# Gate and value projections without sets of seven products, and a new order around them

## The chip, the cores and the metric

The kernel runs on one core of one Trainium2 chip. The metric is the device time of one execution in microseconds; smaller is better. Times given as a median come from several runs of the same program; the profile describes one execution of its own.

## What is computed

Two layers run one after the other. The first is attention with routing by clusters, for 4 batches of 8 heads, 768 positions and a head size of 64. Each query and each key is assigned to the nearest of its head's 16 centroids, and a query sees only the keys of its own cluster:

```python
q_assign = np.argmax(np.einsum('bhsd,hcd->bhsc', q_n, c_n), axis=-1)
k_assign = np.argmax(np.einsum('bhsd,hcd->bhsc', k_n, c_n), axis=-1)
mask = q_assign[:, :, :, None] == k_assign[:, :, None, :]
scores = np.where(mask, scale * (q @ k^T), -1e9)
attn = softmax(scores);  attn_out = attn @ v
```

The second is a gated feed-forward layer over the 3072 tokens that result (512 features in and out, 1536 in between):

```python
x = attn_out.transpose(0, 2, 1, 3).reshape(3072, 512)
gate = 1.0 / (1.0 + np.exp(-(x @ w_gate)))
out = (gate * (x @ w_val)) @ w_out
```

Inputs and output are float32; inside, most products are made in float16.

## The kernel before, in words

**Tiles and stages.** Heads are handled in pairs (four pairs p a batch b), and the queries of a batch in groups (b, gr): two groups of 384 tokens for batches 1 to 3; for batch 0 a group of 256 and one of 512. The work of a pair has these steps:

- Loads of q, k and v into the `nat` tiles. For the first batch, and for the first two pairs of the second, q and k come as one plain transfer a tile (`load_nat`, last part) and are turned by TensorE against an identity matrix (L617, L795, L903); all later ones come in quarters and are turned on VectorE (L595).
- Cluster scores (L687, L835, L948), the largest of each 16 (L556), the comparison with it (L563), and the turning of the resulting one-hot rows (L574) into the augmented tiles `even` and `odd`, which hold 64 rows of q or k and 16 rows of one-hot. One product of 80 rows then gives the score and the mask at once. For the first pairs `place` writes these rows on VectorE directly.
- Attention (`attend`): scores (L1008) into one of two `sc` tiles of two banks each, the exponential on ScalarE (L1032), the product with v (L1059), which also sums the weights; then a reciprocal and a normalisation on VectorE (L1084, L1089), and the turning of the result into `x` by a transposing DMA on SP (L1117) or by TensorE and VectorE (L1097, L1113).

When all pairs of a group are done, `feed` makes the feed-forward layer's first half for that group, and `project` its second half.

**The gate and value projections.** `feed` goes over 12 feature chunks of 128. In the plain form (`proj`, L1422) each chunk has a gate product and a value product, each of four matmuls over 384 tokens into one of three `ring` banks; a tanh on ScalarE (L1585) and a gating on VectorE (L1596) follow. Two chunks so take 16 matmuls of 384 columns.

In the other form, `seven_products`, two feature chunks are made as one set. The set is seen as a product of 2 x 2 blocks: the two halves of the 512 input features against the two kinds, gate and value, and the two halves of the tokens. Seven block products with sums of blocks take the place of eight. Each has four matmuls over 192 columns (L1498), 28 a set. What this needs beside them:

- sums of weight blocks, made once for the chunk pairs 2, 4 and 8 (`sum_up_weights`, L1403, four on VectorE for each);
- differences of blocks of `x`, four on VectorE for each group with sets (L1460), kept in `tb`;
- in each set three copies out of a bank by ScalarE (L1517), three additions by VectorE (L1529), two tanh (L1536) and two gatings (L1544). Later products of a set add to a bank that an earlier product has filled and that has been copied first.

The number of sets goes by group: none in batch 0, 2 and 2 in batch 1, 2 and 3 in batch 2, 3 and 2 in batch 3. In the last group, (3, 1), the sets use `sc` tiles as banks, in the others `ring`. The plain form makes the chunks that remain.

**The projection** (`project`, L1275) uses sums and differences of blocks of its own, on the hidden tile `hT` and the output weights. The change does not touch it.

**What sets the order.** Every step is a task added with `od.add`: an engine, a planned duration, what it needs, the buffers it takes, a due time, and `lat`, the planned delay from its end until others may use its result. `Order.schedule` simulates the engines with these numbers and picks, among the tasks that can start first on an engine, the one with the earliest due time. `Order.transfers` plans the landing of DMAs. After eight rounds the tasks are issued in the planned order, and each engine and each queue then runs its instructions in that order on the chip. So a changed duration, `lat` or due time changes no work, but can change the order on every engine.

The numbers that the change touches:

- in `load_nat`, `lat` of a plain load: 2.0 for the second batch (L497);
- in `place`, the due time of the last two of the eight turned rows of pair 0: 2.0 later than the others (L765);
- in `attend`, `early`: the scores before slot 150 are due 33.5 earlier and their value products 19.5 earlier (L997); a pair and group of batches 1 to 3 has 12 slots, and batch 1 begins at slot 96;
- at the end of `attend`, the reciprocal, the normalisation and the turning of the result are due 7.0 before the block (L1122 to L1136);
- `WT` (L1647): the time from which each weight load may be issued on POOL, and its due time; the first two are those of the first third of the gate and of the value weights.

Of the kernel before, what the change touches and what calls it, by code (L numbers as in the profile page):

```python
# [209 lines left out]
def kernel(  # L210
# [64 lines left out]
    od = Order(BUFS, HEIRS)  # L275
# [17 lines left out]
    WP = (2, 4, 8)  # L293
# [50 lines left out]
    c_ident16 = od.add("POOL", 0.2, lambda: nc.gpsimd.tensor_copy(ident16, ident), [c_ident], due=8)  # L344
# [99 lines left out]
    def load_nat(b, p, nm, eng, due, early=0.0, hold=None, behind=()):  # L444
        src = {"k": k, "q": q, "v": v}[nm]
        buf = natb[b, p, nm] = Buf("late" if b else "nat")
        if isinstance(due, tuple):

            nat[b, p, nm] = []
            for e in range(2):  # L450
                nat[b, p, nm].append(
                    dma(
                        eng,
                        lambda e=e: (buf.tile if e else take(buf))[:, e, :, :],
                        lambda e=e: src[b, 2 * p + e].rearrange("(p c) d -> p c d", c=NCH),
                        0.65, (), due[e], acq=[] if e else [buf], uses=[buf] if e else [],
                        seq=nat[b, p, nm][:], lat={"k": (-0.35, -0.8), "q": (0.0, -0.2)}[nm][e],
                    )
                )
            return  # L460
        if quarters(b, p) and nm != "v":

            parts = src[b, 2 * p : 2 * p + 2].rearrange(
                "h (x t c e) (g f) -> e g t c (h x) f", t=32, c=NCH // 2, e=2, g=2
            )
            nat[b, p, nm] = []
            for a in range(4):
                nat[b, p, nm].append(
                    dma(
                        eng,  # L470
                        lambda a=a: (buf.tile if a else take(buf))[
                            32 * a : 32 * a + 32
                        ].rearrange("p h c d -> p (h c d)").rearrange(
                            "p (c x f) -> p c x f", c=NCH // 2, f=32
                        ),
                        lambda a=a: parts[a // 2, a % 2],
                        0.7 if eng == "POOL" else 0.55, (), due, acq=[] if a else [buf], uses=[buf] if a else [],
                        early=early, seq=nat[b, p, nm][:1], pkt=13, lat=2.0,
                    )
                )  # L480
            return
        held = []
        if hold:

            held.append(
                od.add(
                    "DVE", 0.07, lambda: nc.vector.memset(take(buf)[0:1, 0, 0, 0:1], 0.0), [], -8.7,
                    acq=[buf], seq=hold,
                )
            )  # L490
        nat[b, p, nm] = [
            dma(
                eng,
                lambda: buf.tile if held else take(buf),
                lambda: src[b, 2 * p : 2 * p + 2].rearrange("h (p c) d -> p h c d", c=NCH),
                1.05, held, due, acq=[] if held else [buf], uses=[buf] if held else [], early=early,
                seq=behind, lat=2.0 if b else (0.2 if p == 1 else 1.0),  # L497
            )
        ]

# [41 lines left out]
    aug, masked, shifted, turns, in_turn = {}, {}, {}, [], []  # L542
# [207 lines left out]
    def place(b, p, ohf, tiles, last, due, alloc, c):  # L750


        ev, od_ = aug[b, p]
        rows = [(0, "k", 0), (0, "q", 0), (1, "k", 0), (0, "k", 1), (0, "q", 1), (1, "k", 1)]
        if not p:
            rows += [(1, "q", 0), (1, "q", 1)]
        for n_, (e, nm, h) in enumerate(rows):
            g = tiles.index((nm, h))
            m = od.add(
                "DVE", 0.4,  # L760
                lambda g=g, e=e, nm=nm, h=h: turn_matches(
                    aug[b, p][e].tile[64:96, NM[nm], h * QB : (h + 1) * QB],
                    ohf.tile[32 * g : 32 * g + 32, 32 * e : 32 * e + QB],
                ),
                [last, *alloc], lat=0.02, due=due + 0.3 * n_ + (2.0 if n_ > 5 else 0.0), uses=[ohf, aug[b, p][e]],  # L765
            )
            masked[b, p, e, nm, h] = [c[nm, e, h], m]

        if not p:
            return  # L770
        m = dma(
            "SP", lambda: od_.tile[64:80, NM["q"], :],
            lambda: ev.tile[80:96, NM["q"], :], 0.1,
            [masked[b, p, 0, "q", h][1] for h in range(2)] + alloc, due + 20.0, uses=[ev, od_],
        )
        for h in range(2):
            masked[b, p, 1, "q", h] = [c["q", 1, h], m]
# [205 lines left out]
    def attend(block, at, slot):  # L983


        due = due_at(slot)
# [7 lines left out]
        qb_ = aug[b, p][par]  # L994
        sc, es = Buf("sc"), Buf("es")
        vp = vps[(b * NP + p) % NVP]
        early = slot < 150.0  # L997
        t1 = []
        for i, (e, j) in enumerate(some):
            kb = aug[b, p][j % 2]  # L1000

            def score(i=i, e=e, j=j, kb=kb):
# [17 lines left out]
                    acq=[] if i else [sc], uses=[kb, qb_] + ([sc] if i else []),  # L1020
                    seq=scored_last[-1:],
# [24 lines left out]
        first, last = at == 0, at + together == len(UNITS)  # L1046
        if first:
            avb[block] = Buf("av")
        av = avb[block]
# [3 lines left out]
        def value():  # L1053
# [12 lines left out]
        t3 = od.add(  # L1066
            "PE", 0.031 * together * nq,
            value, [t2] + [vload[b, p][e] for e in dict.fromkeys(e for e, _ in some)],
            due + (-4.1 if last else 5.5) - (19.5 if early else 0.0), lat=0.25 if last else 0.0,
            seq=exps[-1:], acq=[av] if first else [], uses=[es] + ([] if first else [av]),  # L1070
        )
# [6 lines left out]
        rr, xn, rg = Buf("rr"), Buf("xn"), Buf("ring")  # L1078
# [25 lines left out]
        xb, xd = x_of[b, gr], xdone[b, gr]  # L1104
# [14 lines left out]
                in_=xn.tile[:, :nq].rearrange("p c d -> p (c d)"),  # L1119
            )  # L1120

        t4 = od.add("DVE", 0.11, rec, [t3], due - 7.0, lat=0.12, acq=[rr], uses=[av])  # L1122
        t5 = od.add("DVE", 0.12 + 0.113 * nq, norm, [t4], due - 7.0, lat=0.14, acq=[xn], uses=[av, rr])
        if not ((b, gr) == (0, 0) and p >= 2 or (b, p) == (0, NP - 1) or block == blocks[-1]):

            xd.append(
                od.add(
                    "SP", 1.4, turn_by_dma, [t5], due - 7.0, seq=xd[:1], lat=0.0 if b else 5.0, dma=0.4,
                    acq=[] if xd else [xb], uses=[xn] + ([xb] if xd else []),
                )  # L1130
            )
            return together
        t6 = od.add("PE", 0.02 + 0.06 * nq, turn, [t5, c_ident16], due - 7.0, lat=0.25, acq=[rg], uses=[xn])
        xd.append(
            od.add(
                "DVE", 0.1 + 0.118 * nq, out_of_bank, [t6], due - 7.0, lat=0.14, seq=xd[:1],  # L1136
                acq=[] if xd else [xb], uses=[rg] + ([xb] if xd else []),
            )
        )
# [242 lines left out]
    wsums_of = {}  # L1382
# [9 lines left out]
    def sum_up_weights(n, fa, due):  # L1392
        g1, g2, v1, v2 = weights(fa)
        s2, s3, s4, s1 = (wss[:, n, i] for i in range(4))
        before = [wload["g"][fa // FPG], wload["v"][fa // FPG]]
        tasks = []
        for to, x, y, op in (
            (s1, v1, v2, ALU.add), (s3, g1, v1, ALU.subtract), (s2, s1, g1, ALU.subtract), (s4, g2, s2, ALU.subtract),
        ):
            tasks.append(  # L1400
                od.add(
                    "DVE", 0.4 if "DVE" == "DVE" else 1.65,
                    lambda to=to, x=x, y=y, op=op: Q2["DVE"].tensor_tensor(to, x, y, op),  # L1403
                    before + tasks[-1:], due, lat=0.12, both=True,
                )
            )
        wsums_of[fa] = [tasks[-1]]

    def feed(b, gr, work):
# [21 lines left out]

        hs_.append(hb)
        free = [h_last[hs_[-3]]] if len(hs_) > 2 else []
        seven = WP[: {(0, 0): 0, (0, 1): 0, (1, 0): 2, (1, 1): 2, (2, 0): 2, (2, 1): 3, (3, 0): 3, (3, 1): 2}[b, gr]]
        if not wsums_of:
            for n, fa in enumerate(WP):
                sum_up_weights(n, fa, 70.0 + 2 * n)
        half = N // 2
        tb, t_tasks = Buf("tb"), []

# [8 lines left out]
        if seven:  # L1449
            for n, (to, x, y) in enumerate(  # L1450
# [6 lines left out]
                def differ(to=to, x=x, y=y, n=n):  # L1457
                    if not n:
# [6 lines left out]
                        acq=[] if n else [tb], uses=[xb] + ([tb] if n else []), seq=free,  # L1465
# [107 lines left out]
        for fc in range(NFC):  # L1573
            due = due_ffn(work)
# [6 lines left out]
            rg, g1 = proj("g", fc, due, free)  # L1581
# [8 lines left out]
            due = due_ffn(work + 0.65 * w)  # L1590
            rv, v1 = proj("v", fc, due, [g1])

            def gated(fc=fc, rv=rv, gt=gt):
# [9 lines left out]
                    acq=[] if fc else [hb], uses=[gt, rv] + ([hb] if fc else []),  # L1603
# [35 lines left out]
    for p_ in range(1, NP):  # L1639
        load_nat(  # L1640
            0, p_, "k", "SP", -8 + p_, hold=[c1] if p_ == 1 else None,
            behind=nat[0, p_ - 2, "v"] if p_ > 1 else nat[0, 0, "k"],
# [1 line left out]
        load_nat(0, p_, "q", "SP", -7.9 + p_, behind=nat[0, p_, "k"])  # L1644
        load_v(0, p_ - 1, "SP", -7.8 + p_, 20.0 + 4.5 * p_, behind=nat[0, p_, "q"])
    load_v(0, NP - 1, "SP", -7.7 + p_, 20.0 + 4.5 * NP, behind=nat[0, NP - 2, "v"])
    WT = (12.5, 16.0, 23.0, 24.0, 29.5, 29.5, 38.0, 29.0, 43.0)  # L1647
    n = 0
    for i in range(NWG):
        for kind in ("g", "v"):  # L1650
# [11 lines left out]
    slot = work = 0  # L1662
# [71 lines left out]
```

## Time and profile before

| | |
|---|---|
| median of 3 runs | 315.62 us (315.27 to 318.08) |
| the profiled execution | 316.29 us |
| its span in the trace | 314.5 us |
| granted TensorE clock, mean | 0.999 |
| instructions | 8301 |

The span runs from the first to the last instruction of the trace; some 1.8 us of the profiled execution lie outside it. PE is TensorE's matmul stream and PEld its weight loads, which overlap it; DVE is VectorE, ACT ScalarE, POOL GpSimd, SP the engine that issues most transfers. A row of a group gives line, engine, operation, what it writes and reads, the shape, the count, then busy time, the mean of one in nanoseconds, and the idle time ahead of it with what ended it. A matmul's duration includes its fill and drain, which overlap the next one, so a product's cost is read from start to start.

### The profile page before, as it was taken

To read this page: it belongs to the slowest core of one execution; us is meant where nothing else is said; L and a number is where in the kernel's file an instruction comes from. 1 tells how busy PE (TensorE), PEld (TensorE's weight loads), DVE (VectorE), ACT (ScalarE), POOL (GpSimd) and SP (SyncE) were. 2 spreads that over 40 slices of the span, in tenths; PEclk is the share of its full clock that TensorE was granted. 3 is DMA by queue.
4 is the path that set the end of the run, shared out by engine and by line. 5 is a ranking of instruction groups with operands and counts; after the bars stand their busy time and mean duration, and the time that the engine had idled before them with its cause. 6 is when DMAs were issued, how large, how long until landed. Compare 5 with 4: busy or idle time off the path is not lost.

```text
span 314.5 us, 8301 instructions
## 1 busy us (share of the span) xinstructions
PE 303.7 (97%) x3251; PEld 223.0 (71%) x3251; DVE 236.5 (75%) x575; ACT 235.0 (75%) x365; POOL 77.5 (25%) x110
## 2 busy tenths in 40 slices
PE   7998899999999999999999999999999999999895
PEld 3677688644578867757776877757777888768674
DVE  4999847799978749885486978977475944786893
ACT  4799899332999979868897768957899778943521
POOL 5897563881011401340002200470000000000000
PEclk9999999999999999999999999999999999999999
DMA  6999999994465886891465683996200022000003
GB/s 216 376 273 150 238 215 121 124 147 68 82 101 105 142 137 176 105 113 40 106 102 88 104 185 94 100 122 59 83 6 15 15 81 79 16 2 36 34 0 133
DMA packets 97430, 34.49 MB, mean 110 GB/s; under 512 B 83136, under 2 KB 93296, under 8 KB 97392
## 3 DMA queue, kind: packets, MB, share of 16 engines
q1 hardware_dynamic: 72048, 24.30, 34.1%
q0 software_dynamic: 24336, 8.65, 27.1%
q10 hardware_dynamic: 1008, 1.02, 0.9%
q8 instruction: 25, 0.41, 0.5%
q14 instruction: 13, 0.11, 0.1%
HBM read 28.34 MB, written 6.29 MB: 110 GB/s over the span
## 4 chain that ended last, share of the span: by engine, by line
PE 83%; ACT 5%; DMA 5%; DVE 5%; issue 1%; DVEq 0%; SPq 0%; ACTq 0%
PE ring L1422 28%; PE sc L1008 17%; PE ring L1275 15%; PE av L1059 9%; PE ring L1498 8%; ACT es L1032 3%; PE sc L687 3%; DMA nat<-in_q_dram 3%; PE sc L1275 2%; DMA out_dram<-out 1%; PE sc L1498 1%; DMA cn<-in_centroids_dram 1%; DVE t L577 1%; DVE even L574 1%; ACT nat L1517 1%
## 5 line engine op out<-in xcount | busy, mean ns | idle before, releaser
L1032 ACT ACTIVATE es<-sc,nbias 128x768 f16<-128x768 f32 (+1 forms) x189 | 168.6, 923 | 18.4 <-PE sc L1008 17.0
L1059 PEld LDWEIGHTS <-es 128*128 128x128 f16 x1152 | 54.9, 97 | 15.0 <-issue 0.2
L1059 PE MATMUL av<-vp,es 128*128 128x65 f16 x1152 | 60.1, 193 | 0.0
L1585 ACT ACTIVATE gt<-ring 128x384 f32<-128x384 f32 (+2 forms) x68 | 34.2, 503 | 33.9 <-PE ring L1422 26.2
L1422 PE MATMUL ring<-x,wv 128*128 128x384 f16 (+2 forms) x272 | 55.3, 325 | 0.1
L1422 PE MATMUL ring<-x,wg 128*128 128x384 f16 (+2 forms) x272 | 55.4, 326 | 0.0
L1596 DVE SCALAR_TENSOR_TENSOR hT<-gt,ring 128x384 f16<-128x384 f32 (+2 forms) x68 | 37.2, 548 | 21.7 <-PE ring L1422 18.1
L650 POOL CAST even<-t 128x768 f16<-128x768 f32 x24 | 20.5, 871 | 118.8 <-DVE t L595 59.7
L1422 PEld LDWEIGHTS <-wv 128*128 128x128 f16 x272 | 25.0, 97 | 15.8 <-issue 0.8
L1422 PEld LDWEIGHTS <-wg 128*128 128x128 f16 x272 | 24.6, 98 | 15.9 <-issue 2.5
L1275 PEld LDWEIGHTS <-hT 128*128 128x128 f16 x294 | 27.1, 98 | 4.6
L1008 PE MATMUL sc<-even 80*128 80x384 f16 (+2 forms) x120 | 26.3, 293 | 1.7 <-ACT es L1032 1.2
L1008 PE MATMUL sc<-odd,even 80*128 80x384 f16 x96 | 26.3, 326 | 0.4 <-ACT es L1032 0.4
L1008 PE MATMUL sc<-odd 80*128 80x384 f16 x96 | 26.4, 325 | 0.1
L1008 PE MATMUL sc<-even,odd 80*128 80x384 f16 (+2 forms) x120 | 26.4, 293 | 0.1
L1008 PEld LDWEIGHTS <-even 80*128 80x128 f16 x216 | 19.9, 98 | 7.5 <-issue 1.6
L1008 PEld LDWEIGHTS <-odd 80*128 80x128 f16 x216 | 19.5, 98 | 7.6 <-issue 2.9
L1529 DVE TENSOR_TENSOR nat<-ring,nat 128x384 f32<-128x384 f32 x26 | 13.9, 551 | 10.1 <-ACT nat L1517 8.6
L1498 PEld LDWEIGHTS <-wss 128*128 128x128 f16 x224 | 19.0, 97 | 3.5 <-issue 1.9
L595 DVE STREAM_TRANSPOSE t<-nat 128x384 f32<-128x384 f32 x40 | 21.4, 556 | 0.0
L334 POOL DMA_DIRECT2D vp<-in_v_dram x24 | 19.7, 833 | 0.1
L1089 DVE TENSOR_TENSOR xn<-av,rr 128x384 f16<-128x384 f32 (+2 forms) x36 | 18.2, 506 | 0.8
(140 smaller groups left out, 456.3 us busy)
## 6 DMA issues: line engine op xcount, KB each, us to landing
out_dram<-out SPq DMA_DIRECT2D x21, 256.0 KB, 2.4
nat<-in_k_dram SPq DMA_DIRECT2D x32, 96.0 KB, 3.0
nat<-in_q_dram SPq DMA_DIRECT2D x32, 96.0 KB, 3.0
odd<-even SPq DMA_DIRECT2D x12, 192.0 KB, 3.2
vp<-in_v_dram POOLq DMA_DIRECT2D x24, 96.0 KB, 4.8
nat<-in_k_dram SPq DMA_DIRECT2D x5, 384.0 KB, 6.9
nat<-in_q_dram SPq DMA_DIRECT2D x5, 384.0 KB, 7.2
nat<-in_v_dram SPq DMA_DIRECT2D x4, 384.0 KB, 6.9
```

The lines of the kernel that those rows point to most:

```text
L334: eng, (0.74 if eng == "POOL" else 0.69) if pkt == 13 else ISSUE[eng], lambda: Q[eng].dma_start(out=out_of(), in_=in_of()),
L595: nc.vector.transpose(t[:, half * QB : (half + 1) * QB].rearrange("p (c x) -> p c x", x=128), blocks_[:, half],)
L650: nc.gpsimd.tensor_copy(t[:, NM[nm], cols], t32[p, nm].tile[:, cols])
L1008: nc.tensor.matmul(out=to, lhsT=kb.tile[0:80, 0, e * QB + j // 2 * 128 : e * QB + (j // 2 + 1) * 128], rhs=qb_.tile[0:80, 1, e * QB + c0 * ...
L1032: i = nc.scalar.activation(to, of, AF.Exp, bias=nbias, scale=D ** -0.5 if quarters(b, p) else scale,).ins
L1059: nc.tensor.matmul(out=av.tile[:, g : g + D + 1], lhsT=es.tile[:, i * N + c * 128 : i * N + (c + 1) * 128], rhs=vp[:, e, j, :], start=firs ...
L1089: nc.vector.tensor_tensor(take(xn)[:, :nq].rearrange("p c (e d) -> p (c e) d", d=D), sums()[:, :, 0:D], rr.tile[:, : 2 * nq].unsqueeze(2). ...
L1275: nc.tensor.matmul(out=ps[:, lo:hi], lhsT=left_()[:, i], rhs=right(i)[:, n0 : n0 + w], start=new and i == 0, stop=i == NFC // 2 - 1, skip_ ...
L1422: nc.tensor.matmul(out=ps[:, :N], lhsT=ws[fc // FPG][:, dcc, fc % FPG, :], rhs=xb.tile[:, dcc, :N], start=(dcc == 0), stop=(dcc == NDC - 1),)
L1498: nc.tensor.matmul(out=ps[:, f], lhsT=w_[:, d, f], rhs=x_()[:, d], start=new and not (f or d), stop=d == 1, skip_group_check=True,)
L1585: lambda rg=rg, gt=gt: nc.scalar.activation(take(gt)[:, :N], rg.tile[:, :N], AF.Tanh, scale=0.5),
L1596: nc.vector.scalar_tensor_tensor(t[:, fc, :N], gt.tile[:, :N], 1.0, rv.tile[:, :N], ALU.add, ALU.mult)
```

## The change

- No group has sets of seven: `seven` is an empty tuple in every group, so all 12 chunks of every group go through the plain form. The weight sums (L1403) and the differences of `x` (L1460) are not made either.
- Plain loads of the second batch are taken by the planner to be usable 3.0 after landing in place of 2.0.
- The last two turned rows of pair 0 are due 4.0 later in place of 2.0.
- Early due times end at slot 144 in place of 150.
- The end of each attention block is due 9.0 ahead in place of 7.0.
- The first gate weights may be issued from 16.5 (before 12.5) and the first value weights from 15.5 (before 16.0).
- The planner makes the order anew from these numbers.

```diff
-                seq=behind, lat=2.0 if b else (0.2 if p == 1 else 1.0),
+                seq=behind, lat=3.0 if b else (0.2 if p == 1 else 1.0),
...
-                [last, *alloc], lat=0.02, due=due + 0.3 * n_ + (2.0 if n_ > 5 else 0.0), uses=[ohf, aug[b, p][e]],
+                [last, *alloc], lat=0.02, due=due + 0.3 * n_ + (4.0 if n_ > 5 else 0.0), uses=[ohf, aug[b, p][e]],
...
-        early = slot < 150.0
+        early = slot < 144.0
...
-        t4 = od.add("DVE", 0.11, rec, [t3], due - 7.0, lat=0.12, acq=[rr], uses=[av])
-        t5 = od.add("DVE", 0.12 + 0.113 * nq, norm, [t4], due - 7.0, lat=0.14, acq=[xn], uses=[av, rr])
+        t4 = od.add("DVE", 0.11, rec, [t3], due - 9.0, lat=0.12, acq=[rr], uses=[av])
+        t5 = od.add("DVE", 0.12 + 0.113 * nq, norm, [t4], due - 9.0, lat=0.14, acq=[xn], uses=[av, rr])
...
-                    "SP", 1.4, turn_by_dma, [t5], due - 7.0, seq=xd[:1], lat=0.0 if b else 5.0, dma=0.4,
+                    "SP", 1.4, turn_by_dma, [t5], due - 9.0, seq=xd[:1], lat=0.0 if b else 5.0, dma=0.4,
...
-        t6 = od.add("PE", 0.02 + 0.06 * nq, turn, [t5, c_ident16], due - 7.0, lat=0.25, acq=[rg], uses=[xn])
+        t6 = od.add("PE", 0.02 + 0.06 * nq, turn, [t5, c_ident16], due - 9.0, lat=0.25, acq=[rg], uses=[xn])
...
-                "DVE", 0.1 + 0.118 * nq, out_of_bank, [t6], due - 7.0, lat=0.14, seq=xd[:1],
+                "DVE", 0.1 + 0.118 * nq, out_of_bank, [t6], due - 9.0, lat=0.14, seq=xd[:1],
...
-        seven = WP[: {(0, 0): 0, (0, 1): 0, (1, 0): 2, (1, 1): 2, (2, 0): 2, (2, 1): 3, (3, 0): 3, (3, 1): 2}[b, gr]]
-        if not wsums_of:
-            for n, fa in enumerate(WP):
-                sum_up_weights(n, fa, 70.0 + 2 * n)
+        seven = ()
...
-    WT = (12.5, 16.0, 23.0, 24.0, 29.5, 29.5, 38.0, 29.0, 43.0)
+    WT = (16.5, 15.5, 23.0, 24.0, 29.5, 29.5, 38.0, 29.0, 43.0)
```

## The prediction

> **What bounds the kernel now.** I read the page from the engine totals down, then the stretches, then the chain.
>
> ```profile
> PE 303.7 (97%) x3251; PEld 223.0 (71%) x3251; DVE 236.5 (75%) x575; ACT 235.0 (75%) x365; POOL 77.5 (25%) x110
> PE 83%; ACT 5%; DMA 5%; DVE 5%; issue 1%; DVEq 0%; SPq 0%; ACTq 0%
> ```
>
> PE is busy 97% of the span and is 83% of the chain that ended last; DVE and ACT stand at 75%. An average hides stages, so the stretches come next (span, PE, PEld, DVE, ACT, POOL, clock, DMA):
>
> ```profile
> 20.00:30.00 10.00, 9.09 (x136) 7.22 (x135) 9.36 (x26) 9.65 (x12) 9.55 (x14) 1.00 1.16 186
> 30.00:40.00 10.00, 8.10 (x120) 6.61 (x117) 8.59 (x24) 8.76 (x11) 5.23 (x7) 1.00 1.21 229
> ...
> 150.00:160.00 10.00, 10.00 (x122) 8.09 (x120) 5.29 (x11) 9.33 (x16) 0.00 (x0) 1.00 0.53 115
> ...
> 270.00:280.00 10.00, 9.69 (x106) 7.21 (x105) 6.89 (x16) 7.75 (x15) 0.00 (x0) 1.00 0.05 11
> 280.00:290.00 10.00, 9.70 (x83) 7.64 (x82) 7.86 (x19) 3.03 (x7) 0.00 (x0) 1.00 0.01 2
> 290.00:300.00 10.00, 9.20 (x75) 6.54 (x74) 7.74 (x19) 5.23 (x13) 0.00 (x0) 1.00 0.15 54
> ```
>
> Between 40 and 270 us almost nothing of PE is free (the quoted 150 to 160 is typical). There the time is the sum of what PE is given; work taken from DVE or ACT gives nothing back. Two places differ. From 20 to 40 us PE lacks 0.9 and 1.9 us while ACT and DVE are nearly full. From 270 to 300 us it lacks 0.31 + 0.30 + 0.80 = 1.41 us: the end of the last batch, where little attention is left to fill a wait. The granted clock is 1.00 in all of them, so the clock enters no sum.
>
> **The change part by part.** *The products.* The loads of the line that makes the sets of seven give their number, and pieces of the chain give the pitch of both kinds:
>
> ```profile
> L1498 PEld LDWEIGHTS <-wss x224: 95/98/101, 122.2 to 295.2; 128*128 128x128 f16 x112
> L1498 PEld LDWEIGHTS <-wg x112: 95/98/102, 121.8 to 290.7; 128*128 128x128 f16 x112
> L1498 PEld LDWEIGHTS <-wv x56: 95/98/100, 126.5 to 296.9; 128*128 128x128 f16 x56
> 154.37 0.99 PE ring L1498 x12
> 297.19 4.55 PE ring L1422 x28
> ```
>
> 224 + 112 + 56 = 392 matmuls of 192 columns: 28 in a set (seven products of four), 14 sets. Twelve take 0.99 us in a row, 82.5 ns each, so a set is 28 x 82.5 ns = 2.31 us. The eight half products that the change puts in their place are, as the kernel writes them, 16 matmuls of 384 columns (gate and value, two feature chunks, four each); 28 of them take 4.55 us, 162.5 ns each, so one product of four takes 0.65 us and the four of them 2.60 us. The change costs PE 14 x 0.29 = **+4.1 us**, and where PE is full, all of it is on the path. Both prices are measured in this trace and in the same stages.
>
> Here a rule speaks against this term. The Trainium skill, "TensorE: Matmul & The Clock Gate", section "LDWEIGHTS (loading the stationary operand)", gives a load of 128 columns P/1.2, about 107 ns. If matmuls went no faster than their loads, a set would cost more than its eight products and removing it would gain. The trace disagrees: the loads last 98 ns each, yet twelve pairs pass in 0.99 us, so loads overlap each other as well as the matmuls. It stays below as a rival with the trace's own 98 ns.
>
> *What goes with the sets on DVE and ACT.*
>
> ```profile
> L1529 DVE TENSOR_TENSOR nat<-ring,nat 128x384 f32<-128x384 f32 x26 | 13.9, 551 | 10.1 <-ACT nat L1517 8.6 <-PE ring L1498 1.3
> L1460 DVE TENSOR_TENSOR nat<-x,nat 128x384 f16<-128x384 f16 x12 | 4.2, 347 | 0.1
> L1403 DVE TENSOR_TENSOR wss<-wg,wv 128x512 f16<-128x512 f16 x3 | 1.2, 416 | 0.0
> L1517 ACT COPY nat<-ring 128x384 f32<-128x384 f32 x24 | 12.1, 502 | 0.6 <-PE ring L1498 0.4
> L1536 ACT ACTIVATE nat<-nat 128x384 f32<-128x384 f32 x28 | 15.1, 566 | 0.0
> L1585 ACT ACTIVATE gt<-ring 128x384 f32<-128x384 f32 x44 | 22.1, 502 | 18.4 <-PE ring L1422 15.6 <-ACT es L1032 1.4 <-DVE hT L1596 0.9
> ```
>
> DVE loses 14 x 3 additions of 551 ns (23.1 us), four differences of 347 ns for each of six groups (8.3 us) and twelve weight sums of 416 ns (5.0 us): 36 us. ACT loses 14 x 3 copies of 502 ns (21.1 us), and its 28 tanh read a bank at 502 in place of 566 ns (1.8 us): 23 us. The 28 gatings stay. I price all this at **nothing** by itself: PE's own queue hides it from 40 to 270 us. It counts only where PE waited for it, which is the next term.
>
> *The waits inside the sets.* PE in the last group, in order of time (start, length, what, idle before it):
>
> ```profile
> 278.13 0.81 PE L1422 MATMUL ring<-x,wg 128*128 128x384 f16 x4
> 279.19 0.33 PE L1097 MATMUL ring<-ident,xn 128*128 128x128 f16 x3 [0.25 <-DVE hT L1544]
> 288.74 0.81 PE L1422 MATMUL ring<-x,wg 128*128 128x384 f16 x4
> 289.85 0.49 PE L1498 MATMUL sc<-nat,wss 128*128 128x192 f16 x4 [0.30 <-ACT p L1517]
> 290.83 0.49 PE L1498 MATMUL sc<-nat,wss 128*128 128x192 f16 x4
> 291.83 0.49 PE L1498 MATMUL sc<-nat,wss 128*128 128x192 f16 x4 [0.50 <-DVE nat L1529]
> 293.13 0.49 PE L1498 MATMUL sc<-nat,wv 128*128 128x192 f16 x4
> 293.86 0.49 PE L1498 MATMUL sc<-x,wss 128*128 128x192 f16 x4 [0.24 <-ACT nat L1517]
> 294.19 0.81 PE L1422 MATMUL ring<-x,wg 128*128 128x384 f16 x4
> 295.07 0.49 PE L1498 MATMUL sc<-nat,wss 128*128 128x192 f16 x4
> ```
>
> A set's later products wait for an ACT copy and a DVE addition of its earlier ones. Start to start, less the pitch: 288.74 to 289.85 is 1.11 - 0.65 = 0.46; 290.83 to 291.83 is 1.00 - 0.33 = 0.67; 293.13 to 293.86 is 0.40; 294.19 to 295.07 is 0.23. Together 1.76 us. At 278.13 a turn waits behind a set's gating on DVE: 1.06 - 0.65 = 0.41, of which I take the marked 0.25. Eight products have no such exchange; their bounds are 0 (the waits stay as waits for a free bank) and -2.2 us. I take **-2.0**, because the 28 products from 297.19 run back to back in the same group with the same three "ring" banks. What is late next there is tanh and gating, 502 and about 550 ns, each shorter than the 650 ns of a product. Elsewhere in the sets the exchange is covered by scores and value products; any small gaps I leave out.
>
> *The second batch's first loads and the start.*
>
> ```profile
> 26.79 8.49 DMA nat<-in_q_dram
> 33.77 0.49 PE L1008 MATMUL sc<-odd,even 80*128 80x384 f16 x2
> 35.41 0.52 PE L617 MATMUL ring<-ident,nat 128*128 128x128 f32 x3 [1.15 <-DMA nat<-in_q_dram]
> 38.15 0.32 PE L1008 MATMUL sc<-odd,even 80*128 80x384 f16 x1 [0.41 <-ACT es L1032]
> 36.30 4.52 ACT L1032 ACTIVATE es<-sc,nbias 128x768 f16<-128x768 f32 x5 [1.10 <-PE sc L1008]
> ```
>
> The first row is a piece of the chain: the q load is issued at 26.79 and lands at 35.28; the planner had placed its turn on PE 1.15 us too early, and scores queued behind that turn left ACT idle 1.10 us. With the load taken to land 1.0 us later, the turn goes behind about as much other PE work. Bounds: -1.15 (all of it goes) and 0 (the load itself comes later too, or the next wait takes over); ACT was nearly full here and PE waits for it at other points. I take **-0.6**, the middle.
>
> *What else moves.* The first value weights are now issued ahead of the first gate weights, and both later:
>
> ```profile
> 13.01 0.95 POOL L334 DMA_DIRECT2D wg<-in_moe_w_gate_dram  x1
> 16.13 0.74 POOL L334 DMA_DIRECT2D wv<-in_moe_w_val_dram  x1
> DMA to landing us min/median/max: 9.4/10.7/16.9
> 39.53 0.60 PE L1422 MATMUL ring<-x,wg 128*128 128x256 f16 x4
> ```
>
> The third row is that of wv. An issue near 17 us that takes as long as the slowest, 16.9, lands near 34, before the first use at 39.5: nothing, with 5.5 us of cover. On POOL the casts that stood behind the first of these issues (0.95 us) come earlier; on the DMA queues the loads on SP get the engines to themselves 3 us longer. The normalisations due two units earlier, the two transposes of the first pair due two later (370 ns each) and the scores from slot 144 that lose their early due time reorder DVE, SP and PE where PE is full; the first two could touch the start. I take zero and keep plus or minus 1 us, the nearest rows being PE's gaps of 1.15 and 0.41 us there.
>
> **Sum:** 4.1 - 2.0 - 0.6 = **+1.5 us**. The profiled execution took 316.29 us, 1.8 more than its span of 314.5; it would become 317.8 and the span 316.0. It stood 0.7 above the median of 315.62, and from the median I forecast **317.1 us**.
>
> **The rivals.** *Full price (slower).* In the last group, 279 to 302 us, eight products want a bank each 0.65 us and there are three; a bank is held for its product, then for tanh or gating. If DVE, which also makes the sums for the projection there, lags by more than one product, PE waits for the bank and the 2.0 us come back under another name; with the start no better either, all 4.1 us are lost: 319.7. It passes 1% once less than 0.95 us of my 2.6 are returned. Against it stands the run at 297.19, with the projection's sums already on DVE.
>
> *A late weight (slower).* The gate weights land after 39.5 us, and PE, which has only scores for a saturated ACT, stands. It costs one us for each us beyond the 5.5 of cover; a landing of 27 us in place of 17 would give +1.5 + 4.5 = 321.6. The rows speak against it.
>
> *The start gains more.* The whole 1.15 goes, with the 0.41 us wait for ACT at 38 us and the plus or minus 1 us on the good side: 4.1 - 2.0 - 1.15 - 0.4 - 1.0 = -0.5, 315.1. For it: from 20 to 40 us PE lacks 0.91 + 1.90 = 2.8 us in all.
>
> *Loads as the limit (faster).* At 98 ns a load a set would be 28 x 98 = 2.74 us against 2.60, and its removal -2.0 in place of +4.1: 4.6 us less, 311.0. This is where the skill's load time would lead; the pitch of 82.5 ns speaks against it.
>
> That the sets stay cannot be: an empty tuple leaves no feature chunk in it.
>
> **How the numbers follow.** Forecast 0.53 (its own range 315.6 to 318.6), full price 0.18, late weight 0.07, better start 0.18, loads 0.04. A range of 314.5 to 320.0 holds the forecast, the full price and most of the better start; the rest is about 0.14. One per cent, 3.16 us, is about what a measurement of this kernel tells from no change (its runs lie from 315.27 to 318.08). Faster by more: 0.04, the loads. Slower by more: the full price less its lower edge, 0.14, the late weight 0.06 and the forecast's upper end 0.02, in all 0.22. Within: 0.74.
>
> **What would show it.** The sets' line is gone, and the 384-wide groups of the gate and value products count 112 more matmuls each at a pitch of 162.5 ns. PE's busy time rises by about 4 us less small gaps; DVE falls to about 200 us and ACT to about 212. From 280 to 300 us PE is full. The wait of the turn for the second batch's q load is below 0.5 us. The forecast is wrong if PE's idle time from 270 on is still over 1 us, if the start shows a wait that is not there now, or if the products' pitch changes.

## The result, and the profile after

The changed kernel takes 315.19 us in the median of 20 runs (314.93 to 315.96), against 316.36 us for the kernel before in 20 runs beside it (315.27 to 318.08). The ratio is 0.9965, with a 95% interval from 0.9953 to 0.9976: **1.2 us faster in the medians**, where 1.5 us slower was forecast. The profiled execution took 315.67 us with a span of 313.9, so 0.62 us less than that of before (316.29).

The page's engine totals and its shares of the chain, changed kernel:

```profile
PE 306.5 (98%) x3083; PEld 212.6 (68%) x3083; DVE 206.9 (66%) x497; ACT 220.2 (70%) x323; POOL 76.9 (24%) x110
PE 92%; DMA 3%; DVE 2%; ACT 1%; issue 1%; SPq 0%; DVEq 0%; ACTq 0%
L1422 PE MATMUL ring<-x,wv 128*128 128x384 f16 (+2 forms) x384 | 78.2, 326 | 0.0
L1422 PE MATMUL ring<-x,wg 128*128 128x384 f16 (+2 forms) x384 | 78.1, 326 | 0.0
```

PE is busy 2.8 us longer in a span that is 0.6 us shorter. Gate and value count 112 matmuls more each; the line of the sets is gone. DVE lost 30 us and ACT 15 us of busy time. The stretches (span, PE, PEld, DVE, ACT, POOL, clock, DMA, GB/s):

```profile
20.00:30.00 10.00, 9.46 (x136) 7.71 (x134) 9.14 (x26) 9.75 (x13) 9.66 (x14) 1.00 1.29 168
30.00:40.00 10.00, 9.62 (x145) 8.27 (x143) 7.12 (x19) 10.00 (x14) 5.48 (x8) 1.00 1.23 214
...
150.00:160.00 10.00, 10.00 (x102) 6.56 (x101) 4.04 (x10) 7.88 (x12) 0.00 (x0) 1.00 0.64 132
...
270.00:280.00 10.00, 10.00 (x90) 6.43 (x88) 4.84 (x10) 4.57 (x8) 0.00 (x0) 1.00 0.00 0
280.00:290.00 10.00, 10.00 (x77) 7.38 (x76) 7.08 (x15) 2.94 (x6) 0.00 (x0) 1.00 0.01 2
290.00:300.00 10.00, 10.00 (x64) 5.99 (x62) 6.53 (x19) 3.92 (x8) 0.00 (x0) 1.00 0.14 53
```

From 30 to 40 us PE has 1.5 us more than before, and from 270 to 300 us it is full. The chain over the last batch's end (start, length, what) shows how full:

```profile
276.32 5.91 PE ring L1422 x36
282.22 1.31 PE sc L1275 x12
283.53 1.30 PE ring L1422 x8
284.83 3.27 PE sc L1275 x30
288.11 13.00 PE ring L1422 x80
301.11 0.66 PE ring L1275 x6
```

Eighty matmuls of the last group pass in 13.00 us, 162.5 ns each, with nothing between them. The Trainium skill, "TensorE: Matmul & The Clock Gate", section "Back-to-back issue gap", gives N/2.4 + 2.5 ns as the gap of a single isolated matmul at the full ("warm") clock, which by estimate is 162.5 ns for 384 columns and 82.5 ns for 192; for a stream of weight loads and matmuls, which this is, it says that the formula is too high at large N and gives about 131 ns at N=512. The trace agrees with the formula and not with the figure for a stream: 13.00 us over 80 here, 0.99 us over 12 for the sets of before, and 216 ns from start to start (median of 99) for the matmuls of 512 columns in both kernels.

**An account of PE's gaps.** A matmul of 384 columns lasts 326 ns in the trace, and the next one can start 162.5 ns after it. So busy time hides a gap that is shorter than the rest of the matmul before it, and shortens a longer one: the 0.46 us at 289.85 us before are marked as 0.30. I therefore took PE's timeline: for each run of matmuls of one shape, the time to the next run's start, less count times the shape's pitch, is a gap. Summed by stage, for the profiled execution of every kernel in this study (the kernels below are named by their edits):

```
                     sets   us     gaps: 0-10 10-40 40-120 120-270 270-   all | us - gaps + 0.29 x sets
before                14  316.29         3.05  5.05   1.09    2.13  2.46 13.79 | 306.56
changed                0  315.67         2.84  3.78   1.23    1.14  0.10  9.10 | 306.57
sets_off               0  317.32         3.06  5.28   1.17    1.16  0.11 10.78 | 306.54
numbers_only          14  314.36         2.76  3.67   0.90    2.11  2.45 11.89 | 306.53
last_off              12  314.61         2.81  4.86   1.06    2.08  0.71 11.53 | 306.56
after_sets_mid        12  313.66         2.87  4.03   0.90    2.08  0.72 10.60 | 306.54
before_wt             14  317.50         3.07  3.84   2.46    3.15  2.47 15.00 | 306.56
before_lat3           14  316.29         2.86  4.95   1.56    1.93  2.46 13.77 | 306.58
after_oldwt            0  316.01         2.91  4.20   1.09    1.15  0.10  9.45 | 306.56
after_sets_15         15  315.96         3.98  4.21   1.10    3.80  0.68 13.77 | 306.54
setsoff_wt             0  315.18         2.96  3.16   1.27    1.13  0.10  8.63 | 306.55
wt_due9               14  314.81         2.93  3.88   0.91    2.13  2.47 12.32 | 306.55
before_look_a         14  315.79         3.07  4.56   1.08    2.12  2.46 13.30 | 306.55
before_look_b         14  316.57         3.17  5.06   1.08    2.29  2.46 14.07 | 306.56
```

The last column is the same within 0.03 us of 306.55 in 14 executions of 12 different kernels. Most of this follows from how a gap is defined: up to the last matmul, the time is the pitches plus the gaps, and whichever pitch is taken for 192 columns, the price of a set moves with it and the column stays constant. The column shows that the rest is alike in all kernels: the other matmuls, and the 3.8 us from the start of the last matmul to the end of the span. It does not show the 0.29 us; that rests on the two pitches. What the table is good for is where the gaps are: before, it has 2.13 us from 120 to 270 us, a stretch of which busy time shows 0.18 us as idle:

```profile
120.00:270.00 150.00, 149.82 (x1656) 113.46 (x1655) 110.99 (x253) 124.18 (x199) 21.65 (x26) 1.00 0.54 85
```

Even between executions of one kernel the gaps differ: the kernel before, profiled three times, has 8.10, 7.63 and 8.23 us of gaps up to 40 us. From before to changed: products +4.06, gaps -4.69 (start and first stage -1.48, middle groups -0.99, last batch's end -2.36, 40 to 120 us +0.14), sum -0.63, measured -0.62.

### The profile page after: what moved, and what is told of

It is laid out like the page before. It is cut to its first block, busy times and chain, and to the rows that moved or that the text cites. A ratio compares the mean times of both kernels' runs of the same rounds, so it can differ in the third digit from the quotient of the medians.

```text
span 313.9 us, 7851 instructions
## 1 busy us (share of the span) xinstructions
PE 306.5 (98%) x3083; PEld 212.6 (68%) x3083; DVE 206.9 (66%) x497; ACT 220.2 (70%) x323; POOL 76.9 (24%) x110
## 4 chain that ended last, share of the span: by engine, by line
PE 92%; DMA 3%; DVE 2%; ACT 1%; issue 1%; SPq 0%; DVEq 0%; ACTq 0%
PE ring L1422 38%; PE sc L1008 20%; PE ring L1275 15%; PE av L1059 11%; PE sc L687 3%; PE sc L1275 3%; DMA nat<-in_q_dram 2%; ACT es L1032 1%; DMA cn<-in_centroids_dram 1%; PE ring L617 1%; PE ring L795 1%; PE ring L835 0%; DVE hT L1593 0%; SPq L334 0%; DVE t L595 0%
## 5 line engine op out<-in xcount | busy, mean ns | idle before, releaser
L1032 ACT ACTIVATE es<-sc,nbias 128x768 f16<-128x768 f32 (+1 forms) x189 | 166.5, 910 | 28.1 <-PE sc L1008 26.7
L1593 DVE SCALAR_TENSOR_TENSOR hT<-gt,ring 128x384 f16<-128x384 f32 (+2 forms) x96 | 52.5, 547 | 61.3 <-PE ring L1422 59.4
L1422 PE MATMUL ring<-x,wv 128*128 128x384 f16 (+2 forms) x384 | 78.2, 326 | 0.0
L1422 PE MATMUL ring<-x,wg 128*128 128x384 f16 (+2 forms) x384 | 78.1, 326 | 0.0
L1582 ACT ACTIVATE gt<-ring 128x384 f32<-128x384 f32 (+2 forms) x96 | 47.0, 489 | 44.1 <-PE ring L1422 25.6
L1422 PEld LDWEIGHTS <-wg 128*128 128x128 f16 x384 | 35.3, 98 | 21.1 <-issue 0.3
L1422 PEld LDWEIGHTS <-wv 128*128 128x128 f16 x384 | 34.4, 97 | 22.4 <-issue 2.5
L1275 PEld LDWEIGHTS <-s 128*128 128x128 f16 x180 | 16.6, 97 | 2.9
L1275 PE MATMUL ring<-nat,hT 128*128 128x256 f16 (+1 forms) x132 | 16.7, 268 | 0.0
```

The source lines that it names most:

```text
L1032: i = nc.scalar.activation(to, of, AF.Exp, bias=nbias, scale=D ** -0.5 if quarters(b, p) else scale,).ins
L1275: nc.tensor.matmul(out=ps[:, lo:hi], lhsT=left_()[:, i], rhs=right(i)[:, n0 : n0 + w], start=new and i == 0, stop=i == NFC // 2 - 1, skip_ ...
L1422: nc.tensor.matmul(out=ps[:, :N], lhsT=ws[fc // FPG][:, dcc, fc % FPG, :], rhs=xb.tile[:, dcc, :N], start=(dcc == 0), stop=(dcc == NDC - 1),)
L1582: lambda rg=rg, gt=gt: nc.scalar.activation(take(gt)[:, :N], rg.tile[:, :N], AF.Tanh, scale=0.5),
L1593: nc.vector.scalar_tensor_tensor(t[:, fc, :N], gt.tile[:, :N], 1.0, rv.tile[:, :N], ALU.add, ALU.mult)
```

## Experiments

Theory A is the forecast's own mechanism with the sizes that the two traces gave: products against gaps, and a start that the planning numbers improve. Theory B puts the gain on VectorE and ScalarE being freed by removing the sets. Times are medians; "before" is the kernel before in runs on the same chip taken between them. Its own median lies between 315.98 and 316.36 us from one series to the next, so medians of different series are compared with about 0.4 us of doubt.

**Sets off, nothing else.**

```diff
-        seven = WP[: {(0, 0): 0, (0, 1): 0, (1, 0): 2, ... (3, 1): 2}[b, gr]]
-        if not wsums_of:
-            for n, fa in enumerate(WP):
-                sum_up_weights(n, fa, 70.0 + 2 * n)
+        seven = ()
```

> The kernel before with no set of seven and nothing else changed; the order is planned anew. Theory A (the sum of TensorE's work and gaps): +4.1 us of products, -2.4 us of waits in the last group, -1.1 us of small gaps in the middle groups, the start as before: about +0.6 us, ratio 1.000 to 1.004, and PE's wait of about 1.1 us for the q load of the second batch is still there. Theory B (the gain comes from removing the sets, by way of free VectorE and ScalarE): the whole gain, ratio about 0.9965, and less idle PE in the start too.

Measured 316.7 us against 316.12, ratio 1.0018 (0.9995 to 1.0041). PE's waits and its timeline at the second batch's q load:

```profile
PE ring L617 <- DMA nat<-in_q_dram: 1.2, 1, 1.2
34.13 0.49 PE L1008 MATMUL sc<-odd,even 80*128 80x384 f16 x2
35.77 0.52 PE L617 MATMUL ring<-ident,nat 128*128 128x128 f32 x3 [1.15 <-DMA nat<-in_q_dram]
```

The wait is there to the hundredth, the gaps from 270 us on fall from 2.46 to 0.11 and those of the middle groups from 2.13 to 1.16. Products +4.06 and these two terms, -3.32, give +0.74. Theory A holds, theory B falls: by itself, removing the sets gains nothing that can be measured. It also ends the rival in which weight loads bound a set: by it this run would have gained about 4 us (2.0 for the loads and 2.0 for the waits).

**The numbers alone, sets kept.**

```diff
 (the changed kernel, with)
-        seven = ()
+        seven = WP[: {...}[b, gr]]   # and the weight sums, as before
```

> The changed planning numbers, with all 14 sets of seven kept. Theory A: the start loses its gaps (-1.3 us from 10 to 40 us), the sets stay as they are: ratio 0.994 to 0.998, with the waits of about 1.8 us in the last group still there. Theory B: no difference, 0.999 to 1.001.

Measured 315.0 us, ratio 0.9967 (0.9953 to 0.998). As theory A has it, the set's waits stay and the start loses its own: the gaps from 10 to 40 us go from 5.05 to 3.67. The issue of the q load on SP, of this kernel and then of before:

```profile
23.64 0.53 SPq L334 DMA_DIRECT2D nat<-in_q_dram  x1
```

```profile
26.79 1.44 SPq L334 DMA_DIRECT2D nat<-in_q_dram  x1
```

The load is issued 3.2 us earlier, ahead of a transposing DMA and a copy of rows that stood before it on SP, and ahead of the weight loads that start near 25 us. No turn waits for it. The profiled execution (314.36 us) was the fastest of the six, so its gaps show the gain at its largest.

**The last group's two sets off, 12 kept.**

```diff
-  ... (3, 0): 3, (3, 1): 2}[b, gr]]
+  ... (3, 0): 3, (3, 1): 0}[b, gr]]
```

> The kernel before without the two sets of the last group alone; 12 sets stay. Theory A: +0.6 us of products, -2.4 us of waits: -1.8 us, ratio about 0.994. Theory B, or if the waits only move to the banks of the eight products: 0 to +0.6 us, ratio 1.000 to 1.002.

Measured 314.9 us against 316.12, ratio 0.9971 (0.9954 to 0.9987). In the trace, the order on PE is that of before up to 284 us. Faster, but about 1 us in place of 1.8. The expectation had counted all 2.4 us from 270 us on; what remains there is one wait:

```profile
270.00:300.00 30.00, 29.69 (x243) 20.60 (x242) 20.32 (x46) 14.09 (x28) 0.00 (x0) 1.00 0.07 22
PE ring L1097 <- DVE hT L1544: 0.2, 1, 0.2
```

That turn waits behind a gating (L1544) of a set of group (3, 0), not of the last group. With it the gap sum there is 0.71, so the last group's own sets were worth 1.75 us of gaps against 0.58 us of products, 1.17 us; the medians lie 1.2 us apart. This run shows that eight products in the last group do not take up the waits again.

**The changed kernel with the 12 sets of the other groups put back.**

```diff
-        seven = ()
+        seven = WP[: {..., (1, 0): 2, (1, 1): 2, (2, 0): 2, (2, 1): 3, (3, 0): 3, (3, 1): 0}[b, gr]]
```

> The changed kernel with the 12 sets of the groups before the last put back. Theory A: against the changed kernel -3.5 us of products and +1.1 us of small gaps, so 2.4 us below it and about 3.5 us below the kernel before, ratio about 0.989. Theory B: the sets cost as much as they save, so no better than the changed kernel, ratio 0.9965 or above.

Measured **313.63 us**, ratio 0.9932 (0.9914 to 0.9949): better than both kernels, 1.6 us below the changed one in the medians and 1.0 us by the two ratios. The sum gives 12 x 0.29 = 3.48 us of products less 1.50 us of gaps (0.94 in the middle groups, 0.62 at the turn behind the set of group (3, 0), the start even): 2.0 us, and the profiled executions lie 2.01 us apart. The 2.4 of the expectation had left out that turn, and its ratio of 0.989 was not reached.

**Three sets in each of the five groups, 15 in all.**

```diff
+        seven = WP[: {..., (1, 0): 3, (1, 1): 3, (2, 0): 3, (2, 1): 3, (3, 0): 3, (3, 1): 0}[b, gr]]
```

> The changed kernel with three sets of seven in each of the five groups (1, 0) to (3, 0), 15 in all, and none in the last group. By the sum: three sets more than in the run with 12, each -0.29 us of products and about +0.08 us of small gaps: 0.6 us below that run, about 313.0 us, ratio 0.991. If ScalarE and VectorE are the limit by then: no better than 0.993.

Measured 314.71 us, ratio 0.9951 (0.9933 to 0.9969): 1.1 us worse than with 12, where 0.6 better was expected; the intervals of the two ratios overlap a little. PE's waits name a new one, and the middle stretch shows the loss:

```profile
120.00:270.00 150.00, 148.94 (x1689) 115.19 (x1686) 115.50 (x260) 125.25 (x205) 21.91 (x26) 1.00 0.51 85
PE ring L1422 <- DMA x<-xn: 0.5, 1, 0.5
PE sc L1008 <- ACT es L1032: 0.6, 2, 0.4
```

The gaps from 120 to 270 us are 3.80 in place of 2.08 us: 1.7 us for three sets that save 0.87. (The profiled executions lie further apart, 2.3 us, because this one has 1.1 us more gaps in its first 10 us, before any set.) Over the whole stretch DVE and ACT are not full (115.5 and 125.3 of 150 us), but stage by stage they nearly are:

```profile
120.00:130.00 10.00, 9.87 (x123) 8.10 (x120) 9.41 (x23) 10.00 (x19) 4.17 (x5) 1.00 0.68 152
190.00:200.00 10.00, 9.77 (x113) 7.72 (x112) 9.85 (x24) 8.86 (x16) 2.14 (x3) 1.00 0.37 95
210.00:220.00 10.00, 9.46 (x100) 6.72 (x98) 9.14 (x24) 7.28 (x11) 2.08 (x3) 1.00 1.22 78
```

From 190 to 200 us, where PE newly loses 0.23 us, DVE is busy 9.85 of 10. So a full engine is not ruled out as part of the miss. The largest loss, from 210 to 220 us, is a transposed `x` that lands after the product that needs it; whether another order would avoid it was not tried.

**Which number makes the start better?** Put back one at a time in the changed kernel, the planned landing (2.0), the two late rows (2.0) and the due time of a block's end (7.0) each leave the planned order on PE, VectorE and SP as it is (planned only; these three were not run). Slot 150 in place of 144 reorders some scores near there. What is left is the time of the first two weight loads. Theory W takes the gain to come from that; theory L, from the planned landing.

```diff
-    WT = (12.5, 16.0, 23.0, ...)
+    WT = (16.5, 15.5, 23.0, ...)
```

> The kernel before with the issue times of the first two weight loads changed and nothing else. In its order the second batch's late q load stands two places earlier on SP, ahead of a transposing DMA and a copy of rows. Theory W (the start's gain comes from the weights' times by way of this order): the load is issued near 24 us, PE's wait for it (1.15 us before) is below 0.3 us, ratio 0.995 to 0.998. Theory L (the gain comes from the planned landing of the load): ratio 0.999 to 1.001 and the wait stays.

Measured 317.57 us, ratio 1.0031 (1.0014 to 1.0047): *slower*, though the start did what theory W said. The load is issued at 24.24, nobody waits for it, and the gaps from 10 to 40 us fall from 5.05 to 3.84. But new ones open at 59 and 64 us. PE in order of time:

```profile
59.27 0.81 PE L1422 MATMUL ring<-x,wg 128*128 128x512 f16 x3
60.32 0.38 PE L1422 MATMUL ring<-x,wg 128*128 128x512 f16 x1 [0.23 <-DVE x L1113]
64.08 1.03 PE L1422 MATMUL ring<-x,wv 128*128 128x512 f16 x4
65.37 0.81 PE L1422 MATMUL ring<-x,wg 128*128 128x512 f16 x3 [0.27 <-DVE hT L1596]
```

PE waits for a copy of `x` and for a gating on VectorE; from 40 to 270 us the gaps are 2.4 us more than before. So this number alone does not carry the gain while the sets are kept.

```diff
-    WT = (12.5, 16.0, 23.0, ...)
+    WT = (16.5, 15.5, 23.0, ...)
-    (reciprocal, normalisation, turning)  due - 7.0
+    (reciprocal, normalisation, turning)  due - 9.0
```

> The kernel before, all sets kept, with the changed weight times and the attention block's end due 9.0 ahead. Theory D (with the sets on VectorE the weights' times alone moved the waits to 59 and 64 us, and the earlier due time takes them away): PE's gaps between 50 and 70 us fall from 1.65 to below 0.5 us, ratio 0.995 to 0.998. Otherwise the waits stay and the ratio is 1.001 to 1.004.

Measured 314.88 us, ratio 0.997 (0.9958 to 0.9982). With the normalisations ahead, the gaps from 50 to 70 us fall from 1.65 to 0.27 us, those from 40 to 270 us return to 3.0, and the start's gain remains. Up to 99 us the order on every engine is that of the run with all the numbers and the sets kept, so the other numbers add nothing to the start. With sets, these two numbers together are enough, and the weights' times alone are not; the due time alone was not run.

```diff
-        seven = WP[: {...}[b, gr]]
+        seven = ()
-    WT = (12.5, 16.0, 23.0, ...)
+    WT = (16.5, 15.5, 23.0, ...)
```

> The kernel before with no sets of seven and the changed issue times of the first two weight loads; the four other numbers as before. Its order differs from the changed kernel's only in some scores near slot 150. Theory W (without the sets the weights' times carry the start's whole gain): ratio 0.996 to 0.998, 1.1 to 1.8 us below the run with the sets off alone. Theory S (several numbers have to act together): ratio 1.000 to 1.003.

Measured 315.31 us against 315.98, ratio 0.9983 (0.9974 to 0.9992). Its median is 1.4 us below that of the run with the sets off alone and 0.1 us from the changed kernel's. The ratio lies just outside the range written down; the kernel before itself ran faster beside it (315.98 against 316.36), which may be why. In the traces, the order on every engine up to 100 us is that of the changed kernel. Without the sets, the weights' times are enough.

By which way they do it is less clear, because they change more than the q load's place: PE's order differs from 15 us on. POOL around 14 us with the sets off and the old times, then with the new ones:

```profile
13.43 0.95 POOL L334 DMA_DIRECT2D wg<-in_moe_w_gate_dram  x1
14.43 2.10 POOL L521 CAST vp<-nat 128x384 f16<-128x384 f32 x4
```

```profile
13.34 2.20 POOL L521 CAST vp<-nat 128x384 f16<-128x384 f32 x4
15.48 0.95 POOL L334 DMA_DIRECT2D wv<-in_moe_w_val_dram  x1
```

With the old times the casts of v stand behind the issue of a weight load, and PE's first product with v waits 0.67 us for one; with the new ones the casts start 1.1 us earlier and that wait is gone, together with the 1.15 us for the q load. In these two profiles the gaps up to 40 us fall from 8.34 to 6.12 us. No run moved the q load or the casts alone.

```diff
-                seq=behind, lat=2.0 if b else (0.2 if p == 1 else 1.0),
+                seq=behind, lat=3.0 if b else (0.2 if p == 1 else 1.0),
```

> The kernel before with the second batch's plain loads taken to be usable 3.0 after landing, nothing else. The order on SP up to 60 us stays as before; some turns of these loads stand later on PE. Theory L: the wait of 1.15 us for the q load goes, ratio 0.995 to 0.998. Theory W: the load is issued near 27 us and lands near 35 as before; the turn waits less, but ratio 0.998 to 1.001.

Measured 316.16 us against 316.28, ratio 0.9991 (0.9973 to 1.001), the median as with 2.0. PE's wait for the load:

```profile
PE ring L617 <- DMA nat<-in_q_dram: 0.3, 1, 0.3
```

0.9 us of that wait is gone, yet the gaps from 10 to 40 us are 4.95 against 5.05: several gaps of 0.1 to 0.4 us between 29 and 40 us took its place, while the marked waits for ACT did not grow (1.4 us against 1.6). So the line that the change names first does not carry the gain. Its 12 runs lie closer together than those of before, from 315.86 to 316.87.

```diff
 (the changed kernel, with)
-    WT = (16.5, 15.5, 23.0, ...)
+    WT = (12.5, 16.0, 23.0, ...)
```

> The changed kernel with the issue times of the first two weight loads of before, all else as changed. The q load stands on SP where it stood before. Theory W: the start loses its gain, ratio 1.000 to 1.003, runs spread over 2 us or more as in the kernel before. Theory L: the gain stays, ratio 0.996 to 0.998, and no wait for the q load.

Measured 316.18 us, ratio 0.9989 (0.9969 to 1.0009), between the two theories: 1.0 us above the changed kernel in the median, but with no wait of PE for the q load, which is issued at 26.82, and with a spread of only 1.2 us. So with the four other numbers changed, the planned landing among them, the wait for the q load goes without the load's earlier place. PE's first product with v waits 0.67 us for a cast here, as with the sets off and the old times. The profiled execution shows 0.35 us of that 1.0 (gaps 9.45 against 9.10). The rest stands in no trace that was taken, and stays open.

**Why the kernel before spreads over 3 us.** Two more profiles of the same program, no edit.

> The kernel before once more, for a second profile. If the spread of its times comes from the landing of the second batch's q load, PE's wait for that load differs from 1.15 us here by about as much as the time differs from 316.29 us.

> The kernel before a third time. The same expectation: time and PE's wait for the q load move together, while the gaps from 120 us on stay within 0.1 us.

They took 315.79 and 316.57 us. PE's waits of the first, then of the second:

```profile
PE av L1059 <- POOL vp L521: 0.9, 1, 0.9
PE ring L795 <- DMA nat<-in_q_dram: 0.5, 1, 0.5
PE ring L617 <- DVE x L1113: 0.2, 1, 0.2
```

```profile
PE sc L1008 <- ACT es L1032: 1.6, 4, 0.7
PE ring L617 <- DMA nat<-in_q_dram: 1.1, 1, 1.1
```

The gaps differ by 0.77 us, the times by 0.78. In the first the turn of the q load waits 0.2 us and not for the load, in the second 1.1 us for it; but the first has a wait of 0.9 us near 15 us, for a cast of v that stands behind the issue of a weight load on POOL, and the second lacks it. So time and the wait for the q load do not move together as was expected: against the first profile of before (316.29 us, wait 1.15) one execution is 0.50 us shorter with the whole wait gone, the other 0.28 us longer with the same wait. The q load is at most one part of the spread; the cast of v is another. The gaps from 120 us on differ by 0.17 us, a little more than was expected. The three kernels that issue this load near 27 us and plan it at 2.0 (before, sets off, last group off) spread over 2.8 to 3.9 us, all others over 0.3 to 1.8 us; beside the last four runs, though, 16 runs of before lay within 1.6 us. So that this load makes much of the spread is possible, not shown.

## Why the prediction was wrong

- **What bounds the kernel: right in kind.** DVE lost 30 us of busy time by the change, and with the sets off alone the kernel is not faster (ratio 1.0018). But that almost nothing of PE is free between 40 and 270 us was read from busy time, and the gaps there come to 3.2 us.
- **The products, +4.1 us: right.** 80 matmuls pass in 13.00 us, at the pitch that the forecast had taken, and 12 of the sets' in 0.99 us.
- **What goes with the sets on DVE and ACT, nothing by itself: right in kind, its estimate of busy time roughly so** (DVE 207 us for 200, ACT 220 for 212). Added up one by one, DVE's instructions do shrink by the 36 us reckoned; the page's busy time counts overlapping ones once and falls by 30. The two engines matter through PE's waits alone.
- **The waits inside the sets, -2.0 us: the step that failed most.** In the last group the 1.76 us went, as forecast, and did not come back as waits for a bank. But the turn at 278 us was counted with the 0.25 us that the trace marks, where the start-to-start gaps around it held 0.63. And "any small gaps I leave out" left out 0.99 us, in gaps of up to 0.3 us each between 120 and 270 us. Busy time had shown only 0.18 us of that stretch as idle. The term measures -3.3 to -3.4 us, beyond its bound of -2.2. So the sets' whole worth is about 0.7 us where the forecast had 2.1.
- **The start, -0.6 us: undersized.** The gaps from 10 to 40 us fall by 1.27 us in the profiles and by 1.38 with the numbers alone, and in medians the numbers give about 1.1 us with the sets; executions of one kernel differ by up to 0.5 us there. The step's mechanism fails as well. The later planned landing alone gains nothing that can be measured (ratio 0.9991, 0.9973 to 1.001), and with the new weights' times the order up to 100 us is the same without it. What carries the gain is the weights' times, with the sets together with the due time of the normalisations. The forecast saw that those times moved POOL's and SP's queues and took zero for it. How the gain comes about, by the q load's earlier place on SP, by the earlier casts of v on POOL or by the other places that move, stays open.
- **What else moves, zero: wrong in detail.** With the sets kept, the weights' times alone cost 1.3 us in the medians, and with the due time of the normalisations beside them the kernel gains 1.1.
- **The rivals.** Full price, a late weight and the loads as limit did not come. The time of the better start did, 315.1 us with a chance of 0.18, but not its sum: it took 2.55 us from the start, where the profiles show 1.3 to 1.5, and the rest came from the sets' gaps. That the times agree is luck. The time lies inside the range and the change inside one per cent, but the sign was that of a rival.

From 1.5 us slower to 0.6 us faster in the profiles is 2.1 us: 1.0 from the small gaps left out, 0.4 from the turn, 0.7 from the start. The medians lie 0.5 us further apart than the profiles, because the changed kernel's profiled execution (315.67) was one of its longer ones; its median is 315.19. The forecast of 317.1 us also started from 315.62, the median of three runs; 20 runs of the kernel before gave 316.36.

## What to carry to other kernels

Where one engine is full, price a change by that engine's start-to-start gaps, not by its marked idle time: a busy engine can lose a microsecond in gaps that no page shows, and fewer columns are worth little if their chain of copies and additions opens such gaps. A sum of work and gaps closes by its definition, so check each price by itself, on a run of instructions without waits. A trick that saves work on the full engine belongs where other work can fill its waits: taken from the last group and kept in the others, 12 sets gave the best kernel here, and with 15 new waits ate the gain. In a planned order, look at which instruction a number moves and past which queue: the number that names a load need not be the one that moves it. One number can move several queues at once, and then its effect is not yet the effect of one of them.

## What the runs showed that was not expected

- A stretch of 150 us that busy time calls 99.9% full held about 1 us of gaps that the sets caused.
- Three further sets cost 1.1 us in the medians though DVE and ACT were busy only 77% and 83% of the stretch from 120 to 270 us; in single stages of it they were nearly full.
- One number, good in the final order, made the kernel before slower by itself (317.57 against 316.28 us, ratio 1.0031, interval above 1), and with a second number beside it the kernel was faster (314.88 against 315.98, ratio 0.997).
- With the old weights' times, the issue of a weight load on POOL stands ahead of the casts of v, and in three of the seven profiles with these times PE's first product with v waited 0.7 to 0.9 us for one; with the new times one profile of seven shows such a wait, of 0.25 us.
